# GpSimd waits behind VectorE's steps on a shared port, fewer DMAs, and a new order, in an attention and convolution kernel on one core

## The chip, the cores and the metric

The kernel runs on one core of a Trainium2 chip. The core has five engines that run side by side, each with its own queue of instructions in order: TensorE (PE: matrix products; its weight loads are listed as PEld), VectorE (DVE), ScalarE (ACT), GpSimd (POOL) and SyncE (SP). They meet by semaphores. DMAs are issued here from SP and from GpSimd. The metric is the device time of one execution in microseconds (us), the median of several.

## What is computed

Eight batches, eight heads, a sequence of 576, and a head width of 64. First an attention with exponential features, then a long convolution over the sequence between two gates:

```python
def phi(x):
    proj = np.einsum('bhsd,df->bhsf', x, w_phi)
    proj = proj - np.max(np.abs(proj), axis=-1, keepdims=True)
    return np.concatenate([np.exp(proj), np.exp(-proj)], axis=-1)
q_p, k_p = (phi(q), phi(k))
kv = np.einsum('bhsf,bhsd->bhfd', k_p, v)
z = np.sum(k_p, axis=2)
num = np.einsum('bhsf,bhfd->bhsd', q_p, kv)
den = np.einsum('bhsf,bhf->bhs', q_p, z)[..., None] + 1e-06
x = (num / den)                    # heads side by side: (8, 576, 512)

proj = x @ w_proj                  # 512 -> 3 * 512
x1, x2, x3 = split(proj)
x2_conv = irfft(rfft(x2, axis=1) * rfft(filter_fft, axis=0), n=576, axis=1)
out = (x1 * x2_conv * x3) @ w_out  # float32
```

## The kernel before

**A list of steps.** The whole kernel is a text, `PLAN`, of 1454 words. A word names a method, its arguments and, behind an `@`, the PSUM bank that it works in; `run` calls them in turn. `ex,k,m,0,1@2` calls `ex("k", "m", 0, 1)` in banks 2 and 3. As every engine has one queue, the order of the words is the order on each engine; semaphores are placed where data or buffers ask for it. Copies out of PSUM and elementwise steps carry the engine's name in the word (`Oe,ACT,4,3`). The sequence is cut in nine classes of 64 positions (position 9t + j), so loads and stores take rows at a stride of nine.

**Constants and the filter (batch 0's time).** `gen_rows`, `gen_part`, `gen_ident`, `gen_back` and `gen_one` make number tables on GpSimd; `gen_cols` and `gen_angles` turn them into angles on VectorE (lines 443, 448 and 437); `gen_sin` makes the Fourier matrices from these on ScalarE; `D1m` and `D1e` mirror one of them; `gen_five` picks columns for a fifth product `H,4`. `filt_load` and `filt_loadt` fetch the filter on SP, `filt_fold` adds and subtracts its halves on GpSimd (line 510), `H` multiplies them by the Fourier matrices, `H_ev` copies the result out.

**Attention, each batch.** `load` (or `loadh`, half a batch) fetches q, k or v on GpSimd's queue; `trh` transposes q and k by DMA on SP (batch 0 does it on TensorE: `pt`, `pte`). `Pk`, `Pkt`, `Qn`, `Qnt` project, VectorE takes absolute maxima (`maxk`, `maxq`, `maxkt`, `maxqt`, line 694), ScalarE exponentials (`ex`, `exkt`, `em`). For q the maximum goes through `mhi`, `mlo` (GpSimd or VectorE, line 718), a transpose `trm` and a copy `trme` into `mT`, and `Pq` subtracts it by a product with the matrix `one`, which holds -1. `vs` scales v on GpSimd (line 736), `KV` and `NE` are the two attention products, `rc` and `xn` divide (lines 779 and 784).

**Convolution, each batch, half a batch later.** `f1` and `f2` fold x (lines 833 and 839), mostly on GpSimd; `trx` transposes it by DMA on SP; `F` is the transform, `X1`, `X2`, `X3` are the projections, `Y1` multiplies by the filter, `m3` adds two products (line 881), `tm` gates, `I` transforms back with `Ie`, `Ip`, `Im` behind it (lines 946 and 949), `ym` gates on GpSimd (line 990), `O` projects out, `Oe` copies to a buffer `o`, `st` stores it in two DMAs (line 1011). Batch 7 ends with `J` and `yj` in place of `I` and `ym`. `RING` says how many buffers a name has: four for `o`, two for `es` and `cv`.

**What VectorE and GpSimd share.** `f1`, `f2`, `m3`, `vs`, `mlo`, `gen_five` and the angles read and write SBUF alone, on whichever engine they stand. In the profile some of them take much longer on VectorE where GpSimd works at the same time.

Of the kernel before, what the change touches and what calls it, by code (L numbers as in the profile page):

```python
# [24 lines left out]
w_load,phi filt_load,2 filt_load,0 filt_load,3 filt_loadt filt_load,1 loadh,k,0,0 gen_part
loadh,k,0,1 gen_ident gen_rows,0 loadh,q,0,0 zeros pt,k,0,0,1@0 pte,ACT,k,0,0,1@0 gen_cols,0
gen_cols,1 gen_angles,0 w_phi pt,k,0,0,0@1 pte,DVE,k,0,0,0@1 Pk,0,0@0 gen_sin,0 gen_angles,2
loadh,q,0,1 gen_sin,2 w_load,proj,0 load,v,0 gen_back Pk,0,1@2 gen_one load,q,1 w_load,proj,2  # L30
filt_fold,POOL,2 gen_rows,1 D1m@4 maxk,0,1@2 maxk,0,0@0 pt,k,0,1,1@6 pt,k,0,1,0@7 pte,DVE,k,0,1,1@6
pte,DVE,k,0,1,0@7 Pk,0,2@6 D1e,ACT@4 ex,k,m,0,1@2 ex,k,p,0,1@2 gen_five,DVE maxk,0,2@6 pt,q,0,0,1@4
pt,q,0,0,0@5 pte,DVE,q,0,0,1@4 pte,DVE,q,0,0,0@5 ex,k,p,0,2@6 Pkt,0@2 maxkt,0@2 ex,k,m,0,2@6
pt,q,0,1,0@4 pte,DVE,q,0,1,0@4 pt,q,0,1,1@5 exkt,m,0@2 pte,ACT,q,0,1,1@5 Pk,0,3@6 ex,k,p,0,3@6
exkt,p,0@2 em,p,0,0 em,m,0,0 ex,k,m,0,0@0 Qnt,0@4 gen_angles,4 maxqt,0@4 maxk,0,3@6 em,p,0,1
ex,k,p,0,0@0 em,m,0,1 gen_sin,4 gen_neg Qn,0,3@4 maxq,0,3@4 trh,q,1,0 trh,q,1,1 Qn,0,2@2 maxq,0,2@2
load,k,1 load,k,2 trh,k,1,1 trh,k,1,0 trh,k,2,1 trh,k,2,0 filt_fold,POOL,1 filt_fold,POOL,0 Qn,0,1@4
Qn,0,0@0 maxq,0,0@0 maxq,0,1@4 H,0@2 H_ev,DVE,0@2 mhi,0 vs,POOL,p,0,0 ex,k,m,0,3@6 H,4@0 H,1@5
mlo,POOL,0 trm,0@4 trme,DVE,0@4 Pq,0,1@3 ex,q,p,0,1@3 ex,q,m,0,1@3 Pqt,0@1 exqt,p,0@1 exqt,m,0@1
H_ev,DVE,1@5 Qn,1,1@6 H_ev,DVE,4@0 maxq,1,1@6 vs,POOL,m,0,1 vs,POOL,p,0,1 H,3@5 H_ev,ACT,3@5  # L40
vs,POOL,m,0,0 Qn,1,0@3 H,2@0 maxq,1,0@3 Pq,0,0@1 ex,q,p,0,0@1 ex,q,m,0,0@1 H_ev,DVE,2@0 gen_angles,3
KV,0,1@6 KVe,ACT,0,1@6 KV,0,0@4 KVe,DVE,0,0@4 Qn,1,3@0 Qnt,1@2 Pq,0,3@6 NE,0,0@4 maxq,1,3@0
gen_sin,3 rc,0,0@4 maxqt,1@2 NE,0,1@0 xn,0,0@4 ex,q,p,0,3@6 ex,q,m,0,3@6 rc,0,1@0 Pq,0,2@2 xn,0,1@0
ex,q,p,0,2@2 ex,q,m,0,2@2 late ptx,0,0@4 ptxe,DVE,0,0@4 f1,DVE,0,0,0 w_load,proj,1 load,q,2 load,v,1
w_load,out f1,POOL,0,0,1 Qn,1,2@0 maxq,1,2@0 mhi,1 f2,POOL,0,0,1 mlo,POOL,1 f2,POOL,0,0,0 NEt,0@4
rct,0@4 ptx,0,1@6 ptxe,DVE,0,1@6 xnt,0,0@4 xnt,0,1@4 NE,0,3@0 rc,0,3@0 xn,0,3@0 Pk,1,1@6 NE,0,2@2
ptxt,0@4 ptx,0,3@0 trm,1@1 rc,0,2@2 xn,0,2@2 trme,DVE,1@1 ex,k,m,1,1@6 ptxte,ACT,0@4 ptxe,ACT,0,3@0
f1,DVE,0,1,1 trh,q,2,0 trh,q,2,1 f1,POOL,0,1,0 f2,POOL,0,1,1 f2,POOL,0,1,0 gen_ends,POOL load,v,2
Pk,1,0@4 ptx,0,2@2 ptxe,DVE,0,2@2 ex,k,p,1,1@6 F,0,0@0 Fe,ACT,0,0@0 Fet,ACT,0,0@0 X1t,0@3
X1te,ACT,0@3 maxk,1,0@4 ex,k,m,1,0@4 ex,k,p,1,0@4 X1,0,3@2 X1e,DVE,0,3@2 F,0,1@0 X1,0,0@3  # L50
X1e,ACT,0,0@3 X1,0,1@2 X1e,ACT,0,1@2 Fe,DVE,0,1@0 F,0,3@4 Fet,ACT,0,3@4 Fe,ACT,0,3@4 Fet,DVE,0,1@0
maxk,1,1@6 F,0,2@0 Fet,DVE,0,2@0 Fe,ACT,0,2@0 Pkt,1@2 maxkt,1@2 X3,0,0@6 tm,0,0@6 Pk,1,2@4
maxk,1,2@4 Pqt,1@0 exkt,m,1@2 exkt,p,1@2 exqt,m,1@0 em,m,1,0 exqt,p,1@0 em,p,1,0 X3,0,1@7 Pk,1,3@2
ex,k,p,1,2@4 maxk,1,3@2 em,m,1,1 ex,k,m,1,2@4 tm,0,1@7 X2,0,2@6 Y1,0,2@6 em,p,1,1 X3t,0@0 X2,0,0@1
X1,0,2@7 ex,k,p,1,3@2 X1e,ACT,0,2@7 tmt,0@0 Y1,0,0@1 X3,0,3@4 tm,0,3@4 X2,0,3@0 Y1,0,3@0
ex,k,m,1,3@2 Pq,1,1@6 Qnt,2@4 maxqt,2@4 X2,0,1@3 Y1,0,1@3 X2,0,4@2 Qn,2,2@4 maxq,2,2@4 ex,q,m,1,1@6
ex,q,p,1,1@6 Pkt,2@0 exkt,p,2@0 exkt,m,2@0 maxkt,2@0 load,k,3 load,k,4 vs,POOL,m,1,0 load,q,3
vs,POOL,m,1,1 vs,POOL,p,1,0 m3,POOL,0,1 Y1,0,4@2 m3,POOL,0,0 load,q,4 KV,1,0@6 KVe,ACT,1,0@6
vs,POOL,p,1,1 Pk,2,1@4 ex,k,m,2,1@4 Qn,2,1@6 maxq,2,1@6 maxk,2,1@4 Pq,1,0@0 ex,q,m,1,0@0
ex,q,p,1,0@0 X3,0,2@2 I,0,0@6 Ie,0,0@6 tm,0,2@2 ex,k,p,2,1@4 I,0,1@0 Im,0,0@6 Ip,0,0@6 Ie,0,1@0  # L60
NE,1,0@2 Pq,1,3@4 ex,q,m,1,3@4 ex,q,p,1,3@4 rc,1,0@2 Ip,0,1@0 Im,0,1@0 ym,POOL,0,0 NE,1,1@6
ym,POOL,0,1 xn,1,0@2 rc,1,1@6 xn,1,1@6 f1,POOL,1,0,0 I,0,3@0 Ie,0,3@0 Im,0,3@0 Ip,0,3@0 I,0,2@2
Ie,0,2@2 Ip,0,2@2 Im,0,2@2 ym,POOL,0,3 ym,POOL,0,2 Qn,2,0@4 Pq,1,2@6 ex,q,p,1,2@6 ex,q,m,1,2@6
trh,k,3,0 trh,k,3,1 trx,1,0 trx,1,1 trh,q,3,1 trh,q,3,0 maxq,2,0@4 Qn,2,3@0 maxq,2,3@0 KV,1,1@2
KVe,ACT,1,1@2 Pk,2,3@4 maxk,2,3@4 Pk,2,2@6 NEt,1@2 rct,1@2 xnt,1,1@2 xnt,1,0@2 O,0,1@0 ex,k,m,2,2@6
ex,k,p,2,2@6 mhi,2 Oe,ACT,0,1@0 ex,k,p,2,3@4 maxk,2,2@6 f1,POOL,1,0,1 f2,POOL,1,0,1 f2,POOL,1,0,0
mlo,DVE,2 em,p,2,1 ex,k,m,2,3@4 O,0,2@1 NE,1,2@2 rc,1,2@2 xn,1,2@2 Oe,DVE,0,2@1 O,0,0@0 trm,2@6
Oe,ACT,0,0@0 trme,DVE,2@6 O,0,3@7 Oe,DVE,0,3@7 F,1,0@2 Fet,ACT,1,0@2 NE,1,3@4 rc,1,3@4 xn,1,3@4
em,m,2,1 Fe,ACT,1,0@2 Pq,2,1@0 Pk,2,0@6 F,1,1@2 ex,q,m,2,1@0 ex,q,p,2,1@0 maxk,2,0@6 em,m,2,0
Fe,ACT,1,1@2 Fet,ACT,1,1@2 trxt,1 trh,k,4,1 X1t,1@4 X3t,1@5 ex,k,m,2,0@6 X1te,DVE,1@4 tmt,1@5  # L70
trx,1,2 trx,1,3 st,0,3 trh,k,4,0 st,0,0 st,0,1 vs,POOL,p,2,1 vs,POOL,m,2,1 f1,POOL,1,1,0
f1,DVE,1,1,1 f2,POOL,1,1,0 KV,2,1@0 Pkt,3@2 maxkt,3@2 f2,DVE,1,1,1 KVe,ACT,2,1@0 load,v,3 exkt,p,3@2
exkt,m,3@2 X1,1,0@5 X1,1,2@4 X1e,ACT,1,2@4 X1e,ACT,1,0@5 F,1,3@0 Fe,DVE,1,3@0 Fet,DVE,1,3@0 F,1,2@2
Fe,ACT,1,2@2 em,p,2,0 ex,k,p,2,0@6 Fet,ACT,1,2@2 X3,1,0@4 X3,1,2@0 tm,1,2@0 tm,1,0@4 X2,1,3@1
Y1,1,3@1 vs,POOL,p,2,0 load,q,5 vs,POOL,m,2,0 load,k,5 Pq,2,0@2 ex,q,m,2,0@2 Pq,2,2@6 ex,q,p,2,2@6
ex,q,m,2,2@6 ex,q,p,2,0@2 Qnt,3@4 maxqt,3@4 X2,1,0@0 Y1,1,0@0 X2,1,4@1 X2,1,2@4 Y1,1,2@4 Y1,1,4@1
m3,POOL,1,1 X1,1,3@0 X1e,ACT,1,3@0 X2,1,1@7 Pqt,2@4 Qn,3,0@2 KV,2,0@0 exqt,m,2@4 exqt,p,2@4
KVe,ACT,2,0@0 Y1,1,1@7 maxq,3,0@2 NE,2,2@6 rc,2,2@6 xn,2,2@6 X1,1,1@4 X1e,ACT,1,1@4 m3,POOL,1,0
NE,2,0@2 rc,2,0@2 xn,2,0@2 NE,2,1@0 rc,2,1@0 xn,2,1@0 NEt,2@6 rct,2@6 xnt,2,0@6 xnt,2,1@6
f1,POOL,2,0,1 f1,POOL,2,0,0 trh,q,4,0 I,1,1@4 Ie,1,1@4 Im,1,1@4 Ip,1,1@4 trx,2,2 trx,2,0 trx,2,1  # L80
trxt,2 st,0,2 Pq,2,3@2 trh,q,4,1 X3,1,1@0 tm,1,1@0 ex,q,p,2,3@2 ex,q,m,2,3@2 I,1,0@6 Ie,1,0@6
X3,1,3@4 Ip,1,0@6 Im,1,0@6 I,1,3@2 tm,1,3@4 Ie,1,3@2 ym,POOL,1,1 Im,1,3@2 Ip,1,3@2 I,1,2@0 Ie,1,2@0
NE,2,3@6 ym,POOL,1,0 Ip,1,2@0 rc,2,3@6 Im,1,2@0 xn,2,3@6 Pk,3,1@4 Qn,3,1@2 maxq,3,1@2 ym,POOL,1,3
ex,k,m,3,1@4 ex,k,p,3,1@4 trx,2,3 Pk,3,2@0 ym,POOL,1,2 X1t,2@6 X3t,2@7 f1,POOL,2,1,1 f1,POOL,2,1,0
ex,k,m,3,2@0 X1te,ACT,2@6 ex,k,p,3,2@0 maxk,3,1@4 tmt,2@7 maxk,3,2@0 f2,DVE,2,1,0 O,1,1@2 yt,ACT,1
Oe,ACT,1,1@2 O,1,0@6 Oe,ACT,1,0@6 O,1,3@7 Qnt,4@2 maxqt,4@2 f2,DVE,2,1,1 f2,DVE,2,0,0 f2,POOL,2,0,1
Qn,3,2@4 maxq,3,2@4 Pk,3,3@0 Oe,DVE,1,3@7 ex,k,m,3,3@0 ex,k,p,3,3@0 O,1,2@6 Oe,ACT,1,2@6 X1,2,1@2
X1e,ACT,2,1@2 X1,2,0@3 X1e,ACT,2,0@3 maxk,3,3@0 F,2,0@4 Fe,ACT,2,0@4 F,2,3@6 Fe,DVE,2,3@6 F,2,2@2
Fet,DVE,2,3@6 Fet,DVE,2,0@4 em,m,3,1 Fe,ACT,2,2@2 Fet,ACT,2,2@2 load,k,6 vs,POOL,m,3,1 O,1,4@0
Qn,3,3@4 maxq,3,3@4 Pk,3,0@2 em,p,3,1 mhi,3 ex,k,p,3,0@2 trh,k,5,1 st,1,0 F,2,1@6 Fe,DVE,2,1@6  # L90
Fet,ACT,2,1@6 Oe,ACT,1,4@0 trh,k,5,0 st,1,2 st,1,1 st,1,3 st,1,4 X3,2,0@1 X1,2,3@4 X1e,ACT,2,3@4
vs,POOL,p,3,1 mlo,POOL,3 load,v,4 tm,2,0@1 maxk,3,0@2 em,m,3,0 X2,2,0@5 X2,2,2@6 X2,2,4@4
ex,k,m,3,0@2 trm,3@0 trme,ACT,3@0 em,p,3,0 Y1,2,2@6 Y1,2,4@4 vs,POOL,m,3,0 vs,POOL,p,3,0 load,v,5
load,q,6 X2,2,3@7 Y1,2,3@7 Y1,2,0@5 Pq,3,0@0 Pq,3,2@3 m3,POOL,2,1 X1,2,2@6 ex,q,p,3,0@0 ex,q,m,3,2@3
ex,q,p,3,2@3 X1e,ACT,2,2@6 X3,2,3@7 ex,q,m,3,0@0 X3,2,1@5 tm,2,3@7 X2,2,1@2 Pq,3,1@6 ex,q,m,3,1@6
# [971 lines left out]
```

## Time and profile before

| | us |
|---|---|
| median of 3 runs | 324.27 (324.19 to 325.1) |
| the profiled execution | 323.44 |
| its span in the profile | 321.7 |
| TensorE busy | 272.9 (85% of the span) |
| VectorE busy | 272.0 (85%) |
| GpSimd busy | 227.1 (71%) |
| ScalarE busy | 224.3 (70%) |

A busy VectorE can be a waiting one: an instruction that has begun and stands still counts as busy. "L448" is line 448 of the kernel; `out<-in` are tile names. In the table by stages DMA share is a mean over 16 DMA engines and goes above 1 where packets overlap. In the chain of waits each row is a start, a length and what the end of the kernel hung on at that time; "SPq" is SP's queue issuing DMAs. PE's clock is at full speed in nearly the whole span.

### The profile page before, as it was taken

The page shows a single profiled execution, that of the slowest core. Times are in us where ns is not written, and L with a number is a line of the kernel's source. Part 1 is how long each engine was busy: PE and PEld are TensorE (multiplying, and loading weights), DVE is VectorE, ACT ScalarE, POOL GpSimd, SP SyncE. Part 2 cuts the span into 40 slices and gives each one's busy share as a digit, 9 for nine tenths or more (in the row PEclk, how much of TensorE's full clock was granted, in tenths as well). Part 3 has the DMA queues.
Part 4 walks back from the last instruction along what each step waited for, and adds up shares of the span by engine and source line. Part 5 has one row for each costly group of instructions (what it writes and reads, how often), then busy time and mean ns, then how long its engine had stood idle before and what let it go on. Part 6 is the DMA issues. An engine that isn't in the chain of part 4 may idle for free.

```text
span 321.7 us, 10206 instructions
## 1 busy us (share of the span) xinstructions
PE 272.9 (85%) x4263; PEld 199.7 (62%) x4289; DVE 272.0 (85%) x461; ACT 224.3 (70%) x374; POOL 227.1 (71%) x186
## 2 busy tenths in 40 slices
...
GB/s 139 208 209 200 168 136 186 155 206 170 109 142 218 118 120 161 177 193 86 106 144 43 67 120 165 176 41 104 160 89 4 84 60 2 28 142 137 36 4 160
DMA packets 72030, 39.98 MB, mean 124 GB/s; under 512 B 52336, under 2 KB 66800, under 8 KB 71984
## 3 DMA queue, kind: packets, MB, share of 16 engines
...
## 4 chain that ended last, share of the span: by engine, by line
PE 51%; DVE 22%; DMA 9%; ACT 8%; issue 5%; SPq 3%; POOL 1%; ACTq 0%; DVEq 0%
PE ps L889 15%; PE ps L867 9%; PE ps L751 4%; PE ps L942 4%; DVE mq L694 4%; DMA out_dram<-o 3%; PE ps L1001 3%; PE ps L765 3%; DVE mk L694 3%; DVE xn L784 3%; DVE whole L448 2%; DVE T L877 2%; PE ps L849 2%; PE ps L845 2%; PE ps L652 2%
## 5 line engine op out<-in xcount | busy, mean ns | idle before, releaser
L889 PE MATMUL ps<-xT,wproj 128*128 128x256 bf16 x512 | 63.2, 273 | 1.2 <-DVE x1s L930 0.8
L889 PEld LDWEIGHTS <-wproj 128*128 128x128 bf16 x512 | 48.3, 98 | 11.0 <-issue 1.7
L990 POOL TENSOR_TENSOR yT<-cv,x1s 128x576 bf16<-128x576 f32 x28 | 35.5, 1282 | 20.7 <-DVE cv L949 14.0
L694 DVE TENSOR_REDUCE mq<-ps 128x8 f32<-128x1024 f32 (+1 forms) x40 | 43.9, 1108 | 5.9 <-PE ps L625 4.6
L694 DVE TENSOR_REDUCE mk<-ps 128x8 f32<-128x1024 f32 (+1 forms) x40 | 44.2, 1112 | 2.8 <-ACT Ekm L680 0.9
L881 POOL TENSOR_TENSOR T<-T,T 128x1024 bf16<-128x1024 bf16 x15 | 31.7, 2124 | 15.1 <-DVE T L877 15.0
L736 POOL TENSOR_TENSOR vm<-vn,vm 128x1152 bf16<-128x1152 bf16 x16 | 34.4, 2155 | 10.9 <-ACT vm L730 9.8
L736 POOL TENSOR_TENSOR vp<-vn,vp 128x1152 bf16<-128x1152 bf16 x16 | 34.4, 2151 | 6.6 <-ACT vp L730 3.1
L680 ACT ACTIVATE Eqp<-ps 128x1024 bf16<-128x1024 f32 x32 | 32.6, 1027 | 7.5 <-PE ps L658 7.3
L1001 PE MATMUL ps<-wout,yT 128*128 128x512 bf16 x134 | 33.4, 379 | 4.0 <-ACT o L281 1.9
L680 ACT ACTIVATE Eqm<-ps 128x1024 bf16<-128x1024 f32 x32 | 32.7, 1029 | 5.2 <-PE ps L658 4.4
L680 ACT ACTIVATE Ekm<-ps 128x1024 bf16<-128x1024 f32 x32 | 32.9, 1029 | 3.5 <-PE ps L618 3.4
L680 ACT ACTIVATE Ekp<-ps 128x1024 bf16<-128x1024 f32 x32 | 32.8, 1029 | 0.3 <-PE ps L618 0.2
L833 POOL TENSOR_TENSOR SD<-xn 128x512 bf16<-128x512 bf16 x23 | 26.6, 1171 | 6.4 <-DVE xn L784 6.2
L867 PE MATMUL ps<-wproj,XF 128*128 128x512 bf16 x118 | 30.1, 380 | 0.5
L839 POOL TENSOR_TENSOR xf<-SD 128x512 bf16<-128x512 bf16 x24 | 27.8, 1174 | 3.9 <-DVE SD L833 3.3
L281 ACT COPY o<-ps 128x512 f32<-128x512 f32 x27 | 15.6, 595 | 18.2 <-PE ps L1001 12.0
L949 DVE TENSOR_TENSOR cv<-es,ps 128x288 f32<-128x288 f32 x56 | 22.5, 445 | 4.5 <-ACT es L946 2.1
L281 ACT CAST x1s<-ps 128x512 bf16<-128x512 f32 (+1 forms) x31 | 16.7, 551 | 13.1 <-PE ps L889 12.1
L942 PE MATMUL ps<-inv,T 128*128 128x288 bf16 x168 | 24.0, 286 | 2.0 <-issue 1.9
L930 DVE TENSOR_TENSOR x1s<-ps,x1s 128x512 bf16<-128x512 f32 x32 | 21.7, 684 | 4.3 <-PE ps L889 2.9
L1001 PEld LDWEIGHTS <-yT 128*128 128x128 bf16 x144 | 13.2, 97 | 17.5 <-issue 3.4
...
## 6 DMA issues: line engine op xcount, KB each, us to landing
...
```

Of the source, the lines that this page charges most:

```text
L281: self.nc.scalar.copy(dst, src)
L680: self.nc.scalar.activation(e, p, AF.Exp, bias=0.0, scale=1.0 if g == "p" else -1.0)
L694: self.nc.vector.tensor_reduce(out=out, in_=src, axis=AX.X, op=ALU.max, apply_absolute_value=True)
L736: self.eng(eng).tensor_tensor(out=t[:, :, :, 0:64], in0=self.at("vn", b)[:, 2 * X:2 * X + 2], in1=t[:, :, :, 64:65].to_broadcast([128, 2, ...
L833: self.eng(eng).tensor_tensor(out=o[:, :, 2 * i:2 * i + 2, :], in0=x[:, :, 0:2, :], in1=x[:, :, 2:4, :], op=ALU.subtract if i else ALU.add)
L839: self.eng(eng).tensor_tensor(out=o[:, :, 2 * i:2 * i + 2, :], in0=x[:, :, 0:4:2, :], in1=x[:, :, 1:4:2, :], op=ALU.subtract if i else ALU ...
L867: self.mm(self.pb(0), l, w[:, kt, 512:1024], start=(kt == 0), stop=(kt == 3))
L881: self.eng(eng).tensor_tensor(out=Y, in0=Y, in1=self.at(f"T{2 * e + 1}", b), op=ALU.add)
L889: self.mm(o[:, d], w[:, kt, f0 + 128 * m:f0 + 128 * m + 128], y[:, 1, ::-1, ::-1] if d else y[:, 0], start=(kt == 0), stop=(kt == 3))
L942: self.mm(self.pb(e, 0, 288), l, inv[:, 2 * e + i if i < 2 else 4 + e, :], start=(i == 0), stop=(i == 2))
L990: self.eng(eng).tensor_tensor(out=self.at("yT", b)[:, m, 0:SEQ], in0=self.at("cv", 4 * b + m).rearrange("p x h t -> p (x h t)"), in1=self. ...
L1001: self.mm(self.pb(0), y[:, kt, 128 * c:128 * c + 128], w[:, kt, :], start=(kt == 0), stop=(kt == 3))
```

## The change

- **A wait.** After every step, `port` looks at what was recorded. `holder` is the last VectorE instruction of `gen_angles`, or of a step in `PORT` that runs on VectorE (`yt` counts only where it has a VectorE instruction). The first GpSimd instruction of the next step in `PORT` on GpSimd, or of `gen_ident`, `gen_back`, `gen_part` or `gen_rows`, then waits by semaphore for the holder, and the holder is cleared. Sixteen such waits come out; among them `gen_rows,1` behind `gen_angles,2`, `filt_fold,POOL,0` behind `gen_angles,4` and `f1,POOL,0,0,1` behind `gen_angles,3`, and thirteen behind an `f1`, `f2`, `m3` or `vs` of VectorE. Nothing makes VectorE wait for GpSimd.
- **Index rows.** The table `fr` is written by six iotas with contiguous outputs in place of three whose output was strided.
- **One DMA** in place of four per filter tile, two for `w_phi`, and two per store.
- **`one`.** It is a maximum over groups of 32 columns of the identity, on VectorE, instead of six small GpSimd instructions; it now holds 1, and `trme` multiplies by -1.
- **Buffers.** `o` has six, `es` and `cv` three.
- **The order and the engines.** The words are the same 1454 steps in another order, with some on another engine: `gen_five` from VectorE to GpSimd; `m3` on VectorE seven times instead of once; two `vs` and all eight `X1te` on VectorE; `f2` on VectorE five times instead of eight; more of `Fe`, `Fet` and `Oe` on ScalarE (24, 23 and 30 times instead of 19, 21 and 27); `KVe`, `X1e` and `yt` one more each; all `mlo` on GpSimd. The filter loads on SP come in another order, behind `w_phi` as before.

```diff
-RING = {..., 'o': 4, ..., 'es': 2, 'cv': 2, 'yT': 2}
+RING = {..., 'o': 6, ..., 'es': 3, 'cv': 3, 'yT': 2}
+PORT = ("f1", "f2", "m3", "vs", "ym", "mlo", "filt_fold", "gen_ends", "gen_five")
...
     def gen_one(self):
-        g, s = self.nc.gpsimd, self.scr
-        one = s.tile([128, 4, 18], BF16, name="onex")
-        for i in range(4):
-            g.tensor_scalar(out=one[:, i, :], in0=self.idx[:, 0:18], scalar1=-32.0 * i,
-                            scalar2=-1.0, op0=ALU.is_equal, op1=ALU.mult)
-        g.tensor_tensor(out=one[:, 0:2, :], in0=one[:, 0:2, :], in1=one[:, 2:4, :], op=ALU.add)
-        g.tensor_tensor(out=self.at("one"), in0=one[:, 0, :], in1=one[:, 1, :], op=ALU.add)
+        one = self.at("one")
+        x = self.at("ident").rearrange("p (i x) -> p x i", x=32)
+        self.nc.vector.tensor_reduce(out=one, in_=x, axis=AX.X, op=ALU.max)
...
-        g.iota(self.fr[:, :, 0].rearrange("p o f -> p f o"), pattern=[[2, 144], [1, 2]], base=0, **kw)
-        g.iota(self.fr[:, :, 1, 0:16].rearrange("p o f -> p f o"), pattern=[[2, 16], [1, 2]], base=256,
-               **kw)
-        g.iota(self.fr[:, :, 1, 16:144].rearrange("p o f -> p f o"), pattern=[[2, 128], [1, 2]], base=0,
-               **kw)
+        for odd in range(2):
+            g.iota(self.fr[:, odd, 0], pattern=[[2, 144]], base=odd, **kw)
+            g.iota(self.fr[:, odd, 1, 0:16], pattern=[[2, 16]], base=256 + odd, **kw)
+            g.iota(self.fr[:, odd, 1, 16:144], pattern=[[2, 128]], base=odd, **kw)
...
     def filt_load(self, a):
         base = 288 * (a // 2) + 5 * (a % 2)
-        for i in range(4):
-            self.nc.sync.dma_start(out=self.fl[32 * i:32 * i + 32, a, :],
-                                   in_=self.dram["filt"][base + i:base + i + 280:9, :])
+        r = base % 9
+        self.nc.sync.dma_start(
+            out=self.fl[:, a, :],
+            in_=self.dram["filt"].rearrange("(t j) f -> j t f", j=9)[
+                r:r + 4, base // 9:base // 9 + 32, :])
...
     def trme(self, eng, b):
-        self.copy(eng, self.at("mT", b), self.ps16[:, self.bank, 0:128])
+        dst, src = self.at("mT", b), self.ps16[:, self.bank, 0:128]
+        if eng == "ACT":
+            self.nc.scalar.mul(dst, src, -1.0)
+        else:
+            self.nc.vector.tensor_scalar(out=dst, in0=src, scalar1=-1.0, scalar2=None,
+                                         op0=ALU.mult)
...
     def st(self, b, c):
         o = self.at("o", 5 * b + c)
-        for i in range(2):
-            bb, j = (b, (0, 2, 5, 7)[c] + i) if c < 4 else (b - 1 + i, 4)
-            self.nc.sync.dma_start(out=self.out[bb][j:SEQ:9, :], in_=o[64 * i:64 * i + 64, :])
+        if c < 4:
+            j = (0, 2, 5, 7)[c]
+            dst = self.out[b].rearrange("(t j) f -> j t f", j=9)[j:j + 2]
+        else:
+            dst = self.out[b - 1:b + 1].rearrange("b (t j) f -> j b t f", j=9)[4]
+        self.nc.sync.dma_start(out=dst, in_=o)
+    def port(self, f, args, first):
+        new = self.nc.cur_bb.bb.instructions[first:]
+        if f in ("gen_angles", "yt") or (f in PORT and "DVE" in args):
+            own = [i for i in new if i.engine == mybir.EngineType.DVE]
+            self.holder = own[-1].name if own else self.holder
+        elif f in PORT and "POOL" in args or f in ("gen_ident", "gen_back", "gen_part", "gen_rows"):
+            own = [i for i in new if i.engine == mybir.EngineType.Pool]
+            if own and self.holder:
+                self.tc.add_manual_dep(
+                    own[0], self.holder, mybir.DependencyInfo(
+                        mybir.DependencyClass.Sync, mybir.DependencyReason.SCHED_ONLY),
+                    reason="port")
+                self.holder = None
```

The new order in batch 0, as far as the prediction follows it (the last constants, the transposes of batch 0, the first projections, and what stands around `Qn,1,1`):

```diff
+... gen_part gen_ident gen_rows,0 loadh,k,0,1 loadh,q,0,1 loadh,q,0,0 load,v,0 gen_cols,0 w_phi
+gen_one zeros gen_angles,0 gen_angles,2 pt,k,0,0,0@0 pte,DVE,k,0,0,0@0 pt,k,0,0,1@1
+pte,DVE,k,0,0,1@1 Pk,0,1@0 gen_cols,1 gen_sin,0 gen_rows,1 gen_back load,q,1 w_load,proj,1
+gen_sin,2 D1m@2 D1e,ACT@2 gen_five,POOL filt_fold,POOL,2 maxk,0,1@0 ... maxk,0,2@2 gen_angles,4
+... gen_sin,4 Qn,0,2@0 ... trh,q,1,1 trh,q,1,0 w_load,proj,0 w_load,proj,2 load,k,1 load,k,2 ...
+filt_fold,POOL,0 H,0@2 filt_fold,POOL,1 Qn,0,1@4 maxq,0,1@4 H_ev,DVE,0@2 mhi,0 ...
+vs,POOL,p,0,1 mlo,POOL,0 trm,0@4 trme,DVE,0@4 Pq,0,1@4 Qn,1,1@1 ...
```

More of the change, by code (lines that the diff above doesn't have):

```diff
@@ L26 @@
+PORT = ("f1", "f2", "m3", "vs", "ym", "mlo", "filt_fold", "gen_ends", "gen_five")
 PLAN = """
[L27 to L95, printed above, removed]
-ex,q,p,3,1@6 tm,2,1@5 Y1,2,1@2 m3,POOL,2,0 X3,2,2@5 Pkt,4@0 KV,3,1@2 KVe,ACT,3,1@2 tm,2,2@5
```

258 lines of the change are left out of this document (165 added, 93 removed).

## The prediction

> **What bounds the kernel now.** I read the table by stages first, to see where TensorE has nothing to do: it is the busiest engine of the page (272.9 us of 321.7), and nothing of the change alters its work.
>
> ```profile
> core 0: us, PE busy (x) PEld busy (x) DVE busy (x) ACT busy (x) POOL busy (x), PEclk, DMA share, GB/s
> 10.00:20.00 10.00, 6.22 (x65) 4.51 (x60) 9.39 (x19) 8.96 (x16) 8.88 (x19) 1.00 1.19 221
> 20.00:30.00 10.00, 1.23 (x19) 0.87 (x17) 9.89 (x9) 2.68 (x7) 5.34 (x3) 1.00 1.22 205
> 30.00:40.00 10.00, 7.84 (x66) 3.93 (x67) 9.62 (x13) 9.95 (x16) 5.03 (x4) 1.00 1.21 172
> ...
> 300.00:322.00 22.00, 14.18 (x100) 9.62 (x99) 9.31 (x15) 2.25 (x4) 3.54 (x2) 0.91 0.26 60
> ```
>
> The columns after the length are busy times. The stages of this table from 50 to 300 us sum to 234.3 us of TensorE in 250, so 15.7 us are idle there; 25.6 us are idle before 50, and 7.5 after 300 (the span ends at 321.7). In the hole from 20 to 30 VectorE is "busy" with nine instructions. The timeline says with what:
>
> ```profile
> start us, us, engine line op out<-in xcount [idle before <-releaser]
> 18.53 6.98 DVE L448 TENSOR_SCALAR whole<-nr,cols 128x288 int16<-128x288 f32 x1
> 18.57 4.67 POOL L510 TENSOR_TENSOR fe<-fl 128x1024 bf16<-128x1024 f32 x2
> ...
> 23.18 2.15 POOL L736 TENSOR_TENSOR vp<-vn,vp 128x1152 bf16<-128x1152 bf16 x1
> ...
> 28.51 1.04 PE L625 MATMUL ps<-wphi,qT 64*128 64x128 bf16 x16 [8.32 <-DVE mq L694]
> ```
>
> The same L448 form takes 0.42 us at the median. Here it holds on for 6.98, until GpSimd has run two folds and a `vs`: 6.56 us of waiting on something that both engines use. TensorE then waits 8.32 us for the maxima behind it. Last, the chain of waits shows two places where a store sets the pace:
>
> ```profile
> 184.81 0.59 SPq L1011
> 185.40 0.05 issue
> 185.45 3.82 DMA out_dram<-o
> ...
> 189.37 0.59 ACT o L281
> ...
> 283.98 0.60 SPq L1011
> ...
> 285.26 3.94 DMA out_dram<-o
> ...
> 289.77 0.59 ACT o L281
> ```
>
> An `Oe` waits for one of four `o` buffers to be stored, and the store waits for SP, which spends 0.59 us on each half.
>
> **Head, VectorE's queue.** Constants first. The `fr` iotas cost 1.68 + 0.28 + 1.50 = 3.46 us on GpSimd; the six contiguous ones go by the rows for 128x128 (0.26, 0.25, 0.24) and 128x32 (0.15), about 1.3 in all. Bounds: 0.9 and, if order of writing is not what makes them slow, 3.46. The second `loadh,k` issue (0.74) also moves behind them. So `fr`, complete at 7.50 now, is complete at 7.50 - 2.16 - 0.74 = 4.6. From there I add VectorE's durations in the new order: `gen_angles` 0 and 2, 1.5 each (two L443 and one L437 row): 7.6. Two `pte`, 0.48 and 0.41: 8.5. `gen_cols,1`, 3.73 now, less 1.25 that its 1.495 us cast loses beside the iotas (its like takes 0.25): 11.0. One maximum (1.22), a `pte` (0.41), three maxima (3.65): 16.3. `gen_angles,4` without the stall (2.65, from 25.1 to 27.8 now): 18.9. Three `pte` (1.3), two half maxima (1.4), four maxima (4.8): 26.4. `H_ev,0` (1.4): 27.8; it ends at 35.5 now. `gen_five` (1.9) has gone to GpSimd, which is free then; its price there is 1.5 to 3 us by the 64-wide rows of both engines, and it only has to end before `H,4`. VectorE's side of the head therefore gains 7.7 us. ScalarE allows it: 17 us of activations and table loads by their rows, from about 11.5 on, put `mhi` near 27.3.
>
> The wait does its work here: `filt_fold,0` waits for `gen_angles,4` (18.9). Behind it stand both folds (4.7), one `vs` (2.15) and `mlo`, ready at about 26; `mlo` needs the last maximum at 26.4 anyway, so nobody is later for it. The first wait, of `gen_rows,1` on `gen_angles,2` (7.6), has the loads of q for batch 1 and of `w_proj` queued behind it; four issues of 0.77 after 4.6 fill the time to 7.7, so it costs nothing.
>
> One place for the notes. The row: VectorE's instruction started 0.04 us before the fold, and still stood through three GpSimd instructions. The Trainium skill (SBUF — State Buffer, Who interferes with whom) says that whichever of the two issues first has the shared pair for its whole instruction, and the other blocks. By that rule a late VectorE step loses one GpSimd instruction, 2.4 us here, and the forecast below would be some 4 us smaller; the row says 6.56, and the row decides.
>
> **Head, the transfers.** They take most of that back. From 10 to 40 us the DMA share stands above 1. The load of q for batch 1 issues at 13.06 and lands 11.0 us later, at 24.1; its transposes issue at 24.09 and 26.00 and land after 11.5 and 11.0, and `Qn,1,1` starts at 37.28. In the new order this load issues near 9.2, with 2304 KB of GpSimd's loads up to its end in place of 2816 (one `w_proj` third fewer), so at 205 GB/s it lands 2.5 us earlier, 21.6. The filter's 1.2 MB go out early in five issues (0.59 each, not sixteen), which brings no byte less. With the transposes as slow as now the second, which `Qn,1,1` now needs, lands at 21.6 + 1.9 + 11.0 = 34.5. TensorE stands in order there, although `trme` is done at 28.2. After that VectorE has 6.8 us of old rows (two maxima, a half one, `gen_angles,3`, `H_ev,2`, `KVe`, two reciprocals) from 35.1 until the first `xn`: 41.9, against 46.1. I take a gain of 4.2; the ends are 2.5 (the load alone) and 7.7 (no transfer in the way).
>
> **Middle.** Half the store issues: 36 fewer at 0.59. The stall at 185 to 190 ends in 1.85 us of idle TensorE, that at 290 in 0.82; six `o` buffers and one issue per store remove both: 2.7. Port losses of VectorE in the middle: one `m3` of 2.39 (a 512-wide `f1` takes 0.42, so about 0.7 alone), one `mlo` of 1.42 (0.18 alone), one `f1` of 1.27: 1.7 + 1.2 + 0.9 = 3.8. Against this: VectorE gets six more `m3` (4.2 at 0.7) and two `vs` (0.7 to 1.4 each by the same slope), six `X1te` (0.42), and gives up three `f2` (0.42), five `Fe`, three `Oe`, one `KVe`, one `X1e` (0.68), two `Fet` (0.28), two `mlo`: about -1 in all with `gen_one` added (0.3). GpSimd gives up six `m3` (2.12) and two `vs` (2.15) for three `f2` (1.15): 13.6 less. ScalarE gets some 4, under 70% busy, behind TensorE. Thirteen waits stand in the middle; each has GpSimd's next `vs`, `f1`, `f2` or load behind it, and costs nothing while `vs` and `f2` have slack. The waits guard one side only: a VectorE step that comes while GpSimd is inside an instruction still loses up to 2.15. With `vs` and `m3` some such losses come back. Ends: 6.5 gained (2.7 + 3.8), 4 lost (two new losses of 2.1). I take 2.5 gained.
>
> **Tail.** The last copy ends at 315.95, the last two issues at 318.61, the span at 321.7; from 312.37 SP works off the ten half stores of batch 7, one each 0.57 to 0.6. With five issues it keeps up with `Oe`, one each 0.87: copy end, 0.6 issue, and the 3.1 that follow the last issue: 2.0 less. A store of 256 KB in one may land up to 0.8 later than of 128 (at 160 GB/s). All five `Oe` on ScalarE cost 0.59 each against 0.87 of TensorE: hidden. I take 1.5; 0 to 2.
>
> **Sum.** 4.2 + 2.5 + 1.5 = 8.2 from the profiled execution's 323.44 (span 321.7 and 1.74 around it): 315.2. The median of the runs is 0.83 above that execution: 316.
>
> **Rivals.** (a) *The transfers hold the whole head*: q lands no earlier, as filter and q now compete from the start, and only the issue order helps: head 2.5, middle 0, tail 1.5, so 320.3. For it: the share above 1. Against it: the 512 KB fewer. (b) *No transfer in the way*: the 11 us of the transposes were the crowd of loads, and the loads are now done earlier: head 7.7, middle 4, tail 2, so 310.6. For it: the transposes of k, later, land in 3.3 to 5.7. (c) *Slower: VectorE stands behind GpSimd in the middle.* It is 92 to 96% busy in the stages from 60 to 90 and 195 to 265. The eight steps newly given to it (six `m3`, two `vs`) each fall into a GpSimd `vs` or `m3` (2.15), as the one `m3` did and as L448 did for three: 8 x 2.15 = 17.2, against 8.2 + 1.3 gained with the middle's 3.8 kept: 332. It decides from five such hits without slack. For it: the one-sided waits. Against it: of the 20 such steps now, only three lost more than 0.8 after 45 us. (d) *The new order gives back in the middle what the head gains*, a wait being late by 2 us in four of seven batches: 324. That the waits do not keep the port free, though the change says so, is part of (c).
>
> **Chances.** Forecast 0.50, (a) 0.18, (b) 0.16, (c) 0.12, (d) 0.04. Range 308 to 322.5: it takes in (a) and (b) and most of both ends of the head and middle; what lies outside is (c), (d) and a little under 308. Under 0.3% (1 us) this kernel's times cannot be told apart. Faster: 0.50 + 0.18 + 0.16 less a little of (a): 0.83; same 0.05; slower 0.12.
>
> **What would show it.** Head: no VectorE constant over 1 us, `filt_fold` after `gen_angles,4`, and TensorE's wait ahead of `Qn,1,1` named as the transposes. If that wait is missing, (b). Middle: no ScalarE `o` waiting for a store; VectorE `m3` near 0.7, not 2.4 (else (c)). Tail: five stores, the span ending under 5 us after the last copy. I am wrong if TensorE's idle time between the first `xn` and the tail grows beyond 20 us.

## The result, and the profile after

| | us |
|---|---|
| before, median of 4 runs beside it | 324.23 (322.34 to 325.1) |
| after, median of 4 runs | 420.58 (419.25 to 423.03) |
| after / before | 1.299 [1.291, 1.308] |
| the profiled execution after, its span | 421.29, 419.5 |
| TensorE, VectorE, ScalarE, GpSimd busy | 291.4, 260.9, 226.9, 211.3 |

The prediction was 316. VectorE and GpSimd are busy for less time than before, and the kernel takes 96 us more. TensorE is busy 18.5 us longer with the same work, at a mean granted clock of 0.868 for 0.994; the clock is low where it has nothing to do (the rows at 0.54 and 0.50 below). The mean DMA rate fell from 124 to 95 GB/s with the same 40 MB moved, so most of the time is not in the engines' work. A ratio leaves disturbed runs out, so below it can differ from the quotient of two medians. Where two kernels did not share their runs of the kernel before, I compare their ratios.

The table by stages of the kernel after, with the columns of before:

```profile
core 0: us, PE busy (x) PEld busy (x) DVE busy (x) ACT busy (x) POOL busy (x), PEclk, DMA share, GB/s
20.00:30.00 10.00, 2.81 (x36) 1.89 (x34) 6.21 (x9) 7.17 (x15) 2.37 (x2) 1.00 1.21 218
30.00:40.00 10.00, 6.23 (x32) 2.30 (x31) 5.20 (x8) 4.47 (x5) 10.00 (x6) 0.97 1.35 95
...
240.00:250.00 10.00, 0.00 (x0) 0.00 (x0) 0.00 (x0) 0.00 (x0) 0.00 (x0) 0.54 1.02 90
...
396.00:404.00 8.00, 0.00 (x0) 0.00 (x0) 0.00 (x0) 0.00 (x0) 0.00 (x0) 0.50 0.13 51
404.00:412.00 8.00, 0.00 (x0) 0.00 (x0) 0.00 (x0) 0.00 (x0) 0.00 (x0) 0.50 0.13 51
412.00:420.00 8.00, 0.00 (x0) 0.00 (x0) 0.00 (x0) 0.00 (x0) 0.00 (x0) 0.50 0.09 35
```

The last three rows are the reading that matters. Nothing is left but stores, nobody competes with them, and until the end of the span they move at a steady 51 GB/s with a DMA share of 0.13. The share is a mean over 16 engines: 0.13 x 16 is 2.1 engines. The end of before, in the same columns:

```profile
316.00:321.70 5.70, 0.00 (x0) 0.00 (x0) 0.00 (x0) 0.00 (x0) 0.00 (x0) 0.66 0.61 140
```

The packets in the two traces (start, length and size of each) say it directly. In the last 15 us of after two packets of 2 KB are in flight at a time, each for 84 ns, which is 24 GB/s for each; in the last 5 us of before there are 15 at the median, each for 152 ns. At 51 GB/s a store of 256 KB takes 5.1 us, and the four of a batch that look like this take 21. In the middle, from 240 to 250, TensorE, VectorE, ScalarE and GpSimd do nothing at all, while DMAs are under way (share 1.02).

The waits (us in total, times, longest) and two pieces of the chain (start, length) name who stands for it:

```profile
ACT o L284 <- DMA out_dram<-o: 27.5, 4, 17.4
PEld L632 <- DMA qT<-qn: 26.1, 2, 14.1
PE ps L624 <- ACT o L284: 16.2, 1, 16.2
```

```profile
377.31 14.58 DMA out_dram<-o
...
391.97 0.04 ACT o L284
```

ScalarE waits for an `o` buffer to be stored, up to 17.4 us, with six of them; TensorE waits for ScalarE; and TensorE waits for transposes, which are issued on SP as the stores are. In the chain the DMAs have 30% of the span, 9% before.

Last the head, where I had forecast the gain, from the timelines of VectorE, GpSimd and TensorE:

```profile
17.54 0.65 DVE L446 TENSOR_SCALAR whole<-nr,cols 128x288 int16<-128x288 f32 x1
...
27.64 4.64 POOL L510 TENSOR_TENSOR fe<-fl 128x1024 bf16<-128x1024 f32 x2 [8.09 <-DMA fl<-in_moe_filter_fft_dram]
...
45.20 0.61 PE L624 MATMUL ps<-wphi,qT 64*128 64x128 bf16 x8 [8.63 <-DMA qT<-qn]
```

VectorE's constant of 6.98 us is gone (0.65). But the fold, at 18.6 before, now stands 8.09 us for the filter, and `Qn,1,1` for its transposes. The first `xn` starts at 57.97, 11.9 us later than before, where the prediction had it 4.2 earlier.

### The profile page after: what moved, and what is told of

The parts are those of the page before. It is cut to its first block, busy times and chain, and to the rows that moved or that the text cites. A ratio compares the mean times of both kernels' runs of the same rounds, so it can differ in the third digit from the quotient of the medians.

```text
span 419.5 us, 10123 instructions
## 1 busy us (share of the span) xinstructions
PE 291.4 (69%) x4289; PEld 208.3 (50%) x4289; DVE 260.9 (62%) x451; ACT 226.9 (54%) x380; POOL 211.3 (50%) x187
## 4 chain that ended last, share of the span: by engine, by line
PE 45%; DMA 30%; DVE 7%; issue 4%; POOL 3%; SPq 3%; ACT 1%; ACTq 0%; POOLq 0%; DVEq 0%
DMA qT<-qn 14%; PE ps L893 10%; PE ps L871 6%; DMA out_dram<-o 5%; PE ps L1005 5%; DMA qn<-in_q_dram 5%; PE ps L946 5%; PE ps L755 4%; PE ps L769 4%; DMA xT<-xn 3%; DMA xTt<-xnt 3%; PE ps L902 2%; SPq L1018 2%; PE ps L849 2%; PE ps L853 2%
## 5 line engine op out<-in xcount | busy, mean ns | idle before, releaser
L893 PE MATMUL ps<-xT,wproj 128*128 128x256 bf16 x512 | 67.2, 281 | 3.6 <-DVE o L286 3.6
L740 POOL TENSOR_TENSOR vm<-vn,vm 128x1152 bf16<-128x1152 bf16 x15 | 32.2, 2150 | 31.7 <-ACT vm L734 31.7
L284 ACT CAST x1s<-ps 128x512 bf16<-128x512 f32 x26 | 15.3, 592 | 44.0 <-PE ps L893 43.8
L1005 PE MATMUL ps<-wout,yT 128*128 128x512 bf16 x144 | 36.8, 394 | 1.7 <-DVE yT L988 0.8
L740 POOL TENSOR_TENSOR vp<-vn,vp 128x1152 bf16<-128x1152 bf16 x15 | 32.2, 2150 | 7.0 <-DVE T L885 4.6
L624 PE MATMUL ps<-wphi,qT 64*128 64x128 bf16 x256 | 14.7, 244 | 29.3 <-ACT o L284 16.2
L843 POOL TENSOR_TENSOR xf<-SD 128x512 bf16<-128x512 bf16 x27 | 30.8, 1152 | 4.5 <-DVE xf L843 2.7
L885 POOL TENSOR_TENSOR T<-T,T 128x1024 bf16<-128x1024 bf16 x9 | 19.0, 2121 | 25.9 <-DVE T L881 24.0
L624 PEld LDWEIGHTS <-qT 64*128 64x128 bf16 x256 | 9.6, 106 | 35.5 <-issue 26.3
L881 DVE TENSOR_TENSOR T<-ps,HTe 128x1024 bf16<-128x1024 f32 x16 | 19.5, 1220 | 9.2 <-PE ps L871 9.2
```

The lines of the kernel that those rows point to most:

```text
L284: self.nc.scalar.copy(dst, src)
L624: self.mm(self.pb((v + j) % 2, 128 * i, 128 * i + 128), x[r, k, :], w[r, :], True, True)
L740: self.eng(eng).tensor_tensor(out=t[:, :, :, 0:64], in0=self.at("vn", b)[:, 2 * X:2 * X + 2], in1=t[:, :, :, 64:65].to_broadcast([128, 2, ...
L843: self.eng(eng).tensor_tensor(out=o[:, :, 2 * i:2 * i + 2, :], in0=x[:, :, 0:4:2, :], in1=x[:, :, 1:4:2, :], op=ALU.subtract if i else ALU ...
L893: self.mm(o[:, d], w[:, kt, f0 + 128 * m:f0 + 128 * m + 128], y[:, 1, ::-1, ::-1] if d else y[:, 0], start=(kt == 0), stop=(kt == 3))
L1005: self.mm(self.pb(0), y[:, kt, 128 * c:128 * c + 128], w[:, kt, :], start=(kt == 0), stop=(kt == 3))
```

## The experiments

### Which DMA is it?

The patterns as built: a store of `c` below 4 has 2 x 64 x 512 elements on the DRAM side, outermost dimension first, and a filter tile 4 x 32 x 512. The fifth store of a pair of batches merges to 128 x 512. My theory: the outermost dimension sets how many DMA engines carry a transfer, two for a store. The rivals: the new order, or the port waits.

`a1_two_stores` puts back the two DMAs per store, `a3_wide_filter` the four per filter tile and two for `w_phi`, `a2_all_wide` both; `b1_one_store` puts the new store alone into the kernel before.

```diff
 a1, a2 (b1 the other way round):
-        self.nc.sync.dma_start(out=dst, in_=o)
+        for i in range(2):
+            bb, j = (b, (0, 2, 5, 7)[c] + i) if c < 4 else (b - 1 + i, 4)
+            self.nc.sync.dma_start(out=self.out[bb][j:SEQ:9, :], in_=o[64 * i:64 * i + 64, :])
 a2, a3 (and w_phi in two):
+        for i in range(4):
+            self.nc.sync.dma_start(out=self.fl[32 * i:32 * i + 32, a, :],
+                                   in_=self.dram["filt"][base + i:base + i + 280:9, :])
```

> The changed kernel with each store again in two DMAs of 64 rows. Theory: a store whose outermost dimension is 2 is moved by 2 of the 16 DMA engines (0.13 of them busy and 51 GB/s at the end of the changed kernel's span, where nothing but stores runs, against 0.61 and 140 GB/s at the end of the kernel before). Most of the 96 us go: the 27 us after the last copy come down to under 7, the waits of the o buffers (27.5 us) and of the transposes behind the stores go; about 335 us, as the four filter loads still use 4 engines each and hold the head. Rival 1 (the new order and its waits are what is slow): over 390. Rival 2 (a filter's or store's issue count has nothing to do with it, the stores only lengthen the end): about 395, the end alone.

> The changed kernel with the filter tiles again in four DMAs of 32 rows and w_phi in two of 64; the stores stay one DMA each. Theory: the filter loads have an outermost dimension of 4, use 4 engines, and make the first fold wait until 27.6 us and q of batch 1 land at 28.4; with them wide the fold starts near 19 and the whole gains 8 to 10 us in the head: about 411. The stores go on costing some 85. Rival 1 (order and waits): no change, 420. Rival 3 (the filter loads started the trouble, and what is late from then on stays late): under 360.

> The changed kernel with stores, filter tiles and w_phi all in the DMAs of the kernel before; the new order, the waits, the buffers, the iotas and the engines stay. Theory: what is left is the part that the prediction reckoned with (head 4.2, middle 2.5 less what the SP queue saved), so 314 to 322. Rival 1 (order and waits): over 330. If a1 and this differ by 8 to 12 us, that is what the filter loads cost.

> The kernel before with one change: each store one DMA. Theory (narrow stores): much slower, 380 to 420, whatever the order, since four o buffers wait for stores of 10 us and more and the transposes stand behind them on SP; the end alone costs 20 us. Rival 1 (order and waits of the changed kernel are the cause): 320 to 325, the end a little shorter.

| run | median us | to before |
|---|---|---|
| a1_two_stores | 343.29 | 1.059 [1.053, 1.065] |
| a3_wide_filter | 416.32 | 1.288 [1.279, 1.296] |
| a2_all_wide | 338.26 | 1.044 [1.038, 1.050] |
| b1_one_store | 409.01 | 1.262 [1.256, 1.268] |

The store is worth 420.58 - 343.29 = 77 us in the new order and 409.01 - 323.79 = 85 in the old, the filter and `w_phi` 4 to 5, about half of the 8 to 10 that I expected. In `a2` 14.5 us remain for the rest of the change; I had expected it at 314 to 322, so the narrow DMAs are not the whole loss. The end of `b1_one_store`, by stages, and its longest wait:

```profile
390.00:400.00 10.00, 0.00 (x0) 0.00 (x0) 0.00 (x0) 0.55 (x1) 0.00 (x0) 0.50 0.24 75
400.00:407.00 7.00, 0.00 (x0) 0.00 (x0) 0.00 (x0) 0.00 (x0) 0.00 (x0) 0.50 0.10 40
```

```profile
ACT o L281 <- DMA out_dram<-o: 44.2, 8, 11.6
```

The same picture, without new order or waits. It is still open here whether it hurts that a store is one DMA or that its outermost dimension is 2. `d1_t_major` (on the basis of `c2_trh_earlier`, below; batch 7 keeps two DMAs) tells these apart: one DMA, but 64 outermost, for which `ym` writes y with the two rows of a pair side by side.

```diff
 st, batches 0 to 6:
+            dst = self.out[b].rearrange("(t j) f -> t j f", j=9)[:, j:j + 2]
 ym, first 512 columns (the other 64 in a second instruction):
+            out=y[:, 0:512].rearrange("p (c t i) -> p c i t", c=4, i=2), ...
```

> One DMA per store again, but with 64 for the outermost dimension of its address pattern on the DRAM side in place of 2: the columns of y are written with the two rows of a pair side by side, so that the store's 128 partitions go t by t to runs of 4 KB. Batch 7, whose y is written by VectorE, keeps two DMAs. Everything else is the version with both wide patterns and the earlier transpose (328.9 us). If the outermost dimension sets how many of the 16 DMA engines carry a store: 327 to 333 us, and no stretch at a DMA share of 0.13. If it is that a store is one DMA: 28 of 36 stores are, so 60 us or more come back, 385 us or above. The strided write of y on GpSimd (28 times 1.28 us now) may cost up to twice that on GpSimd, which idles 100 us, so 0 to 5 us of the time.

It measured 326.79 us, ratio 1.008 [1.001, 1.015], against 1.0135 [1.004, 1.023] for its basis: no loss, and a gain is not shown, as the intervals overlap. The 28 stores of 36 in question would have cost 60 us or more if one DMA were the trouble. On GpSimd `ym` took 1.16 + 0.31 us in place of 1.28. So it is the outermost dimension. (The new order of rows also makes the contiguous pieces in DRAM 4 KB instead of 2; the two DMAs of `a1` have pieces of 2 KB and are not slow, so that is not it.) The Trainium skill says so too (DMA: Bandwidth & Descriptors, Rules for kernel authors, "Use all 16 engines"): an outermost dimension of a size c below 16 confines a DMA to at most c engines. The trace agrees, with 0.13 x 16 = 2.1 engines.

### What is the rest of the loss?

The chain of waits of `a2_all_wide` in the head, and the same stretch by stages:

```profile
9.10 11.77 DMA qn<-in_q_dram
20.89 2.01 SPq L587
22.90 0.05 issue
22.95 19.44 DMA qT<-qn
42.40 0.05 issue
42.44 0.61 PE ps L623 x8
```

```profile
30.00:40.00 10.00, 0.00 (x0) 0.00 (x0) 0.89 (x2) 1.04 (x2) 4.16 (x4) 0.57 1.40 153
```

One transpose takes 19.44 us, where I had reckoned 11.0, with five GpSimd loads (2.7 MB) issued from 9.9 to 16.8 beside it; TensorE does nothing for ten, and the first `xn` starts at 53.15 (before: 46.04). A second hole, from 110 to 118, ends with `trh,q,3,0`, issued behind SP's other work at 101.72 and landed 16.7 us later. Four edits on `a2_all_wide`:

```diff
 c1: PLAN, from before filt_fold,POOL,0 to before w_load,out
+ w_load,proj,0 load,k,1 load,k,2 w_load,proj,2 trh,k,1,1 trh,k,1,0 trh,k,2,0 trh,k,2,1
 c2: PLAN, behind trh,q,3,1
+ trh,q,3,0
 c3:
-            self.port(f, args, first)
 c4: c1 and c2
```

> a2 (all DMAs wide, new order and waits) with four GpSimd loads (two thirds of w_proj, k of batches 1 and 2) and the transposes of k issued behind the last vs of batch 0 instead of ahead of the first fold. In a2 q of batch 1 lands at 20.9, as forecast, but its second transpose takes 19.4 us, with those loads in flight (landing times 14 to 21 us), and TensorE waits 13.4 us for it at Qn,1,1. Theory (transposes crawl beside GpSimd's loads): with the loads behind it the transposes land in 3 to 6 us, TensorE's wait at Qn,1,1 falls under 3, and the time by 7 to 12: 326 to 331. Rival 4 (the two transposes of q are slow of themselves, whatever runs beside them; or TensorE's in-order wait is taken up later): a2's 338 within 2.

> a2 with one word moved: the second transpose of q of batch 3 right behind the first on SP, ahead of five x transposes, a k transpose and a store. In a2 it issues at 101.7, just after three GpSimd loads (97.4 to 100.9), lands 16.7 us later, and TensorE waits 10.7 us for it at Qnt,3. Theory (transposes crawl beside GpSimd's loads, and this one was put behind them): it lands before the loads start, the wait goes, 8 to 11 us less: 327 to 330. Rival 4 (slow of itself): 338 within 2. Rival 5 (the x transposes now pushed back by it cost the same elsewhere): 335 to 338.

> a2 without any of the sixteen added semaphore waits, all else the same. Theory (the waits are small: they free the head's angles from the folds but TensorE waits there for the transposes anyway, and the middle's steps of 0.42 and 0.73 us lose little): 338 within 3. Rival 1 (the waits hold GpSimd back and are part of a2's 14.5 us): 3 or more faster. Third reading (the waits save VectorE's port losses on the path): 3 or more slower, with a VectorE constant or m3 of over 2 us in the groups.

> c1 and c2 together. Theory: the two waits are apart in time (29 to 42 and 108 to 118 us), so the gains add: 316 to 322, at or under the kernel before; this is what the prediction had reckoned with. Rival 5: no better than the better of c1 and c2.

| run | median us | to before |
|---|---|---|
| c1_loads_later | 343.36 | 1.059 [1.052, 1.066] |
| c2_trh_earlier | 328.85 | 1.014 [1.004, 1.023] |
| c3_no_waits | 338.05 | 1.034 [1.023, 1.046] |
| c4_both | 340.21 | 1.032 [1.022, 1.041] |

`c2` came out as expected: the order of two transposes on SP in batch 3 was worth 9.4 us. `c1` and `c4` missed; `c4`, with times from 333.2 to 345.4, is no better than `c2` alone. In `c1` the transposes of q for batch 1 land in 3.6 and 4.5 us and TensorE's wait for them is gone, but the waits show where it went:

```profile
PE ps L616 <- DMA kT<-kn: 15.8, 1, 15.8
```

Moving k's loads behind q only made k's own transposes late, beside the same loads. `c3` has `a2`'s median; by the ratios it is 0.01 lower, with intervals that overlap. Here, then, no gain from the port waits is seen while the transposes hold the head, and a small cost is not excluded. `d2_loads_later`, on `c2`, moves only what is not needed soon:

```diff
 d2: PLAN, to behind load,v,1
+ load,k,2 w_load,proj,0 w_load,proj,2
 and to before trh,q,2,0
+ trh,k,2,0 trh,k,2,1
```

> The version with both wide patterns and the earlier transpose (328.9 us), and of the five GpSimd loads that are in flight while q of batch 1 is turned, three issued later, behind v of batch 1: w_proj 0, w_proj 2 and k of batch 2 (1.6 of 2.7 MB), with the two transposes of that k. k of batch 1 and its transposes stay, which the run that moved both k's made late by 15.8 us. If the transposes of batch 1 are slow because the loads' bytes share the engines with them: 1.6 MB at the 200 GB/s of that stretch are 8 us, the PE's wait of 12.2 us falls below 5, and the time to 319 to 324 us. If the transposes are slow beside any load: the wait goes down by less than 3, and the time stays at 326 to 329.

It measured 323.42 us, ratio 0.993 [0.984, 1.002], and in its chain the transpose lasts:

```profile
22.68 6.76 DMA qT<-qn
```

6.76 us for 17.10 in `c2`: with 1.6 of 2.7 MB out of the way, a transpose of the same tile takes two fifths of the time. Some k transposes were moved along with the loads, but they were not what slowed it: in `a2` the first transpose of q is issued at 20.89 and takes 12.9 us, and SP issues no k transpose before 34.07. What slowed it is the loads beside it; in what way they do is not shown.

### What are the port waits worth?

`d3_old_order` is `a2_all_wide` with the words of before's `PLAN`, `d4_old_order_no_waits` the same without `port`. With six `o` and three `cv` buffers one store and three `ym` of that order come too late for their buffer and carry another chunk's values; the amount of work is the same.

> The changed kernel with both wide patterns, and the order of before in place of its own: what is left of the change is the port waits, the contiguous index rows, phi first in the code and six o buffers. If the new order is what costs the 14 us of that version (338.3): 318 to 325 us, and below the kernel before by as much of the head's 6.9 us constant as was on the path (0 to 7 us). If the waits or buffers cost it: 333 us or above.

> The same with the order of before, and without the port waits: contiguous index rows and buffers alone. If the waits help in the order of before: 2 to 7 us above the run that has them, with a VectorE constant of 6 to 7 us in the head again. If the head of the order of before is held by its transfers: the two agree within 2 us, whatever VectorE does.

320.85 us, ratio 0.990 [0.983, 0.997], and 324.21, ratio 1.000 [0.994, 1.006]. The two timelines (VectorE, then GpSimd), first without and then with the waits:

```profile
17.68 7.53 DVE L435 SCALAR_TENSOR_TENSOR turn<-nr,cols,whole 128x288 f32<-128x288 f32 x1
...
18.13 4.67 POOL L508 TENSOR_TENSOR fe<-fl 128x1024 bf16<-128x1024 f32 x2
22.73 2.16 POOL L739 TENSOR_TENSOR vp<-vn,vp 128x1152 bf16<-128x1152 bf16 x1
```

```profile
17.66 0.52 DVE L435 SCALAR_TENSOR_TENSOR turn<-nr,cols,whole 128x288 f32<-128x288 f32 x1
...
20.05 4.65 POOL L508 TENSOR_TENSOR fe<-fl 128x1024 bf16<-128x1024 f32 x2 [2.13 <-DVE turn L435]
24.66 2.15 POOL L739 TENSOR_TENSOR vp<-vn,vp 128x1152 bf16<-128x1152 bf16 x1
```

GpSimd gives 2.13 us and VectorE gets 7. The next runs repeat this with buffers that fit the order, and put the parts together: `e1` is `d3` with before's buffers, `e2` with seven `o`, three `es` and two `cv`, `e3` is `e2` with `d1`'s stores, `e4` the new order with `c2`, `d2` and `d1`.

> The order of before, its four o, two es and two cv buffers, its two DMAs per store and four per filter tile; of the change there remain the port waits and the contiguous index rows. The waits took a VectorE step of 7.53 us to 0.52 in this order, and the evictions of the filter's spectrum began 7.0 us earlier. If that is worth at the end what the pair of runs with other buffers gave: 319 to 322 us, 2 to 5 us below the kernel before. If the buffers had given the gain: 323 to 325.

> The same with seven o buffers and three es. In the kernel before, ACT and VectorE waited for a store's buffer 2.7 us in all, which the prediction took for a gain of as much. If these waits lie on the path: 1 to 3 us below the run with the old buffers. If they only move to the next wait of the same engine: within 1 us of it.

> The order of before, the port waits, the contiguous index rows, seven o buffers, and one DMA per store with 64 for the outermost dimension (batch 7 keeps two): 316 to 321 us, since one wide DMA per store took 2.1 us off in the new order (328.9 to 326.8), by freeing SyncE's queue ahead of the transposes; if that difference was noise, the same as the run with seven o buffers.

> The new order with the transpose of batch 3 moved, three of five early loads later, and the wide one-DMA stores: 320 to 324 us, the 323.4 of the later loads less 0 to 2. If it is above the run of the order of before with the same stores, the new order itself is worth nothing here.

| run | median us | to before |
|---|---|---|
| e1_old_order_old_buffers | 320.75 | 0.991 [0.988, 0.995] |
| e2_old_order_7_o | 321.08 | 0.992 [0.988, 0.996] |
| e3_old_order_t_major | 318.63 | 0.985 [0.979, 0.991] |
| e4_new_order_best | 315.77 | 0.973 [0.968, 0.979] |

With the old order and buffers, the waits, the contiguous rows and the new `one` are worth 2.8 us together; as `d4`, without the waits, is at 1.000, it is the waits. The buffers are worth nothing (ScalarE's waits for a store are 6.5 us in `e1` and 2.3 in `e2`, and the kernel's time is the same). The wide store in one DMA may be worth 2.4 us (`e3` to `e2`), but these intervals overlap. `e4` is below what I expected, and below both kernels: 8.0 us under before, 105 under after. It is 2.9 us under `e3`, which has the same stores and waits, and the intervals do not overlap, so the new order with its transfers put right is worth something. Two runs took `e4` apart, `f1` without `port`, `f2` with two DMAs per store (it is `d2` again):

> The best version (315.8 us) without its 16 port waits. If they are worth in the new order what they are in the order of before (3.4 us, a VectorE step of 7 us in the head): 318 to 322 us, and a VectorE instruction of more than 2 us beside GpSimd. If the order itself keeps the two engines apart: within 1.5 us of 315.8.

> The best version with two DMAs per store and y written in natural order, which is the run with later loads again, in more rounds (323.4 us then, from 318.9 to 326.9). If the wide store in one DMA gives 2 us: 317 to 319 us. If it gives the 7.7 us that lay between the two runs: 322 to 325.

`f1`: 321.04 us, ratio 0.990 [0.987, 0.994]; the waits are worth 0.990 - 0.973 = 1.7%, 5.5 us, here. Its timelines of VectorE and GpSimd have the collision again:

```profile
17.63 2.46 DVE L445 TENSOR_SCALAR whole<-nr,cols 128x288 int16<-128x288 f32 x1
20.12 2.48 DVE L434 SCALAR_TENSOR_TENSOR turn<-nr,cols,whole 128x288 f32<-128x288 f32 x1
...
17.38 4.91 POOL L507 TENSOR_TENSOR fe<-fl 128x1024 bf16<-128x1024 f32 x2 [3.38 <-DMA fl<-in_moe_filter_fft_dram]
```

`f2`: 324.84 us from 318.9 to 329.61, ratio 0.990 [0.985, 0.994]: 1.6% above `e4` by the ratios. So the wide store in one DMA gives some 5 us here, where the intervals do not overlap, and about 2 in the pairs `c2`, `d1` and `e2`, `e3`, where they do. Why the size differs between the pairs, and where in `f2` the 5 us lie, was not settled.

The best version, `e4`, by stages, and what VectorE does in its head:

```profile
20.00:30.00 10.00, 7.89 (x71) 3.95 (x69) 8.88 (x13) 8.95 (x17) 9.04 (x6) 1.00 1.24 195
30.00:40.00 10.00, 6.03 (x207) 4.80 (x209) 6.89 (x11) 7.36 (x11) 6.51 (x7) 1.00 0.77 124
...
50.00:300.00 250.00, 238.63 (x3737) 176.20 (x3757) 216.68 (x341) 183.75 (x314) 179.00 (x160) 0.99 0.70 119
```

```profile
27.86 0.23 DVE L728 TENSOR_SCALAR mT<-ps 128x128 bf16<-128x128 bf16 x1 [0.73 <-PE ps L719]
```

TensorE, 1.23 us busy from 20 to 30 before, is busy 7.89; from 50 to 300 it is idle 11.4 us in place of 15.7.

## Why the prediction was wrong, and where it was right

**The step that failed** is the pricing of the fewer DMAs. The prediction had "Half the store issues: 36 fewer at 0.59", and for the tail "A store of 256 KB in one may land up to 0.8 later than of 128"; of the filter it had "The filter's 1.2 MB go out early in five issues", "which brings no byte less". It counted issues and bytes, and took the rate for given. The rate is what the edit changed: two engines carry a store, and four a filter tile (from 10 to 26 us at most four of the filter's packets are in flight, up to 12 in `a2_all_wide`). The issues did get fewer, but they did not get cheaper, since SP now stood behind the slow stores. Its last five issues, and the ten of before:

```profile
387.68 17.06 SPq L1018 DMA_DIRECT2D out_dram<-o  x5
```

```profile
312.37 6.24 SPq L1011 DMA_DIRECT2D out_dram<-o  x10
```

The tail, where 0 to 2 us were to be gained, has 26 us from the last copy to the end of the span (before: 5.75), and the middle filled with waits for stores and for the transposes behind them: 77 to 85 us in all. None of the rivals named it, so the range could not hold it. The rule of the Trainium skill quoted above (DMA: Bandwidth & Descriptors, Rules for kernel authors) spoke against this change: read against the diff's `"(t j) f -> j t f"`, which puts j with its two rows outermost, it gives 2 of 16 engines for a store, as the trace shows. The profile before had most of the rest: its end moved 140 GB/s at a share of 0.61, so 14 GB/s per busy engine, and two of those would have been 29 GB/s. Measured were 51, as each packet takes 84 ns with two in flight and 152 with 15.

**VectorE's queue: right to under a microsecond, once the DMAs are wide.** In `a2_all_wide` the fold started at 18.88 (forecast 18.9), `H_ev,0` ended at 27.0 (27.8), and `trme` was done at 28.4, in `e4` at 28.1 (28.2). In the kernel as changed the filter held all this back: the fold at 27.64, `trme` at 35.68.

**Head, the transfers: the load right, the transposes mis-sized.** q of batch 1 landed at 20.9 in `a2_all_wide` (forecast 21.6), at 28.4 in the kernel after, beside the narrow filter. "With the transposes as slow as now", 11.0 us, was the term that was off: 19.4 us, because the new order puts five loads beside them. With three of these moved it was 6.8 in `d2` and 5.9 and 6.7 in `e4`, where the wait at `Qn,1,1` fell to 0.53 us and the first `xn` started at 40.2 (forecast 41.9, before 46.0). So rival (b)'s reason, "the crowd of loads", was the true one, but the change had not moved the crowd away.

**Middle: the port right, the buffers and the order not.** VectorE's `m3` is at 0.73 us in the mean (forecast 0.7), here in `e4`, and 0.73 in the kernel after too. That does away with rival (c), and not by the waits alone: without them, in `f1`, the mean is 0.90, so the order already keeps most of these steps clear of GpSimd. The row of `e4`:

```profile
L883 DVE TENSOR_TENSOR T<-T,T 128x1024 bf16<-128x1024 bf16 x7 | 5.1, 730 | 0.1
```

"Six `o` buffers and one issue per store remove both: 2.7" was nothing for the buffers (`e1`, `e2`). What I passed over is the place of `trh,q,3,0` in SP's queue, 9.4 us. That is rival (d), a wait late in the middle, which I had priced at 2 us a batch.

**Tail.** Its 2.0 us were not tried: batch 7 kept its two DMAs in `e4`, and the span ends 5.7 us after the last copy, as before.

**The sign of being wrong** that the prediction named came up: from 50 to 300 us TensorE is idle 62.4 us (15.7 before), and ScalarE waited for stores.

That 315.77 us is so near to the predicted 316 is luck: it belongs to another kernel, with the stores, three loads and a transpose changed.
